# Buffers placed by the time they die, a shorter last routing and column-half sums in a kernel of pooled attention and soft mixture of experts

## The chip, the core and the metric

The kernel runs on one core of a Trainium2 chip. A core has a matrix engine (PE), a vector engine (DVE), an activation engine (ACT), a general engine (POOL), a queue that issues transfers (SP), and 16 DMA engines which all transfers share. The metric is the device time of one execution in microseconds; lower is better.

## What is computed

Everything is float32. Attention goes over 32 memory slots which are pooled from 576 tokens for each of 8 x 8 heads; its output is never formed for its own sake, but goes through a mixture of 8 experts with 4 slots each.

```python
a    = softmax(phi, axis=tokens)                # phi: 8 x 8 x 576 x 32
k_m  = einsum('bhsm,bhsd->bhmd', a, k)          # k, v: 8 x 8 x 576 x 64
v_m  = einsum('bhsm,bhsd->bhmd', a, v)
attn = softmax(q @ k_m.T / 8, axis=-1)
x    = (attn @ v_m) as 4608 tokens x 512
logits = x @ moe_phi                            # 4608 x 32
d    = softmax(logits, axis=tokens);  slot_input = d.T @ x      # 32 x 512
slot_out[e] = relu(slot_input[e] @ w1[e]) @ w2[e]               # 8 experts, 512 -> 1024 -> 512
out  = softmax(logits, axis=slots) @ slot_out   # 4608 x 512
```

The weights w1 and w2 are 32 MiB of the 66.65 MB that are read; the output is 9.44 MB.

## The kernel before

All work is added to a list (`add`, L45) with an engine, an estimated cost, the tiles that it reads and writes, and a priority. `Plan.order` (L77) plays the list through with these costs and writes out one order for each engine; nothing is reordered on the chip, so each engine and the SP queue work in that order.

**Attention.** The loop at L926 goes over four pairs of batches (`bp`). A pair loads phi, k, v and q, pools k and v (`pool_phi`, `pool_kv`), and for each of four head groups c does `scores` (L708, products at L716), `softmax` (L737, its result transposed at L777 into a tile of `aTs`) and `logits` (L780, product at L785), all summed into one PSUM bank `lp`. L955 transposes that bank into `L[bp]`.

**Routing.** `route` (L795) takes one pair's logits: a maximum over tokens (reduce L803, PE transpose L810, reduce L815, PE transpose L821), its subtraction (L829) and exp (L837) into `df`; the routing product L849 of `df` with the attention weights `ex` (a tile of `sexs`) and a column of ones; two copies of the result into `wt` on ACT (L861, L865); products L875 and L881 (the second gives the pair's sum of exponentials); a mask on DVE (L890) into `wtb`; and the product L909 with the pooled values `vm`. The pair's maximum goes to `MB` (L834), its sum to `SD` (L901), its slot sums to `SIU` (L922). After the last pair the four results are merged (L969 to L1000): scale by exp of the maximum's difference, add, divide, and write `SIM`, the input of the experts.

**Fills.** `fill` (L472) adds matmuls on ones whose result nobody reads. Twelve of them (L961, `NTAIL`) may go into gaps of PE once the third pair's maximum is there. On the profile they are L476.

**Experts.** `expert_in` (L1088, product L1097) runs w1 of eight experts, `hidden` the relu and a transpose into `hTb` (zeroed by POOL at L1050), `expert_out` (L1135, product L1148) w2. A weight tile is 1 MiB, two for each matrix. The products of `expert_out` accumulate in one PSUM bank over 512 columns; the last tile (`last`, L1139) comes in four quarter loads of 256 KB, and its two column halves go to spare parts of the banks. `slot_sums` (L1063) copies the accumulator to SBUF in column halves (L1070 on DVE, L1075 on ACT) and adds its four partition groups with a product (L1080); it runs once for all but the last tile and once for the last. Then `sr` is formed (L1266, L1271), and the output is products L1280 of the token softmaxes `cT` with `sr`, copies L1302, L1304, L1333, L1335 out of PSUM and transfers L1313 and L1343. `slots` (L1191) forms the token softmaxes, one pair after every second expert.

**Buffers.** Attention tiles live in one arena of 44,288 columns, stacked from the bottom in the order of the `stack` calls (L370 to L395). The 19 weight slots of 2048 columns (`ws`, L1025) lie over the same columns from 5376 up. A load into a slot waits for the last use of every attention tile under it, and for the planner a slot opens only when every tile of the pools under it has been handed out. Two more weight tiles use the area of q (`wqs`). SP issues the loads at L458.

Of the kernel before, what the change touches and what calls it, by code (L numbers as in the profile page):

```python
# [235 lines left out]
def act(n, psum=True):  # L236
    return (0.16 if psum else 0.19) + n / 1200.0
# [15 lines left out]
def kernel(  # L253
# [103 lines left out]
    def stack(shape, n, fifo=False):  # L357

        nonlocal top
        p = area(top, shape, n, (), fifo)  # L360

        p.aps.reverse()
        p.ranges.reverse()
        early.append(p)
        top += sum(c for _, c in p.ranges)
        return p


# [8 lines left out]
    dfs = stack([JN], 2)  # L377
    wts = stack([2, H * M + 1], 2)
# [17 lines left out]


# [10 lines left out]
    NTAIL = 12  # L408
# [31 lines left out]
    dmhs = sb("dmh", [NS, 1], 2)  # L440
    L = [keep(f"L{i}", [P, JN]) for i in range(NBP)]
# [353 lines left out]
    def route(bp, ex, vm):  # L795

        dm1, dmh, df = dm1s.tile(), dmhs.tile(), dfs.tile()
# [36 lines left out]
        add(ACT, act(32), lambda: nc.scalar.copy(MB.ap[:, bp, :], t1.ap[:, :NS]), r=[t1], w=[mbp])  # L834
# [4 lines left out]
        )  # L839
        wp = [b_m.tile(), b_m.tile()]  # L840
        wt, wtb = wts.tile(), wtbs.tile()
# [16 lines left out]
        add(PE, 1.3, f, r=[df, ex], w=wp, also=[wt])  # L858
# [7 lines left out]

        for g in range(2):
            add(ACT, act(HM) + act(1), lambda f=f, g=g: f(g), r=[wp[g]], w=[wt.part(g)])
        wtp = b_m.tile()

        def f():
            for g in range(2):
                for a in range(2):
                    x = NS * (2 * g + a)
                    nc.tensor.matmul(  # L875
                        wtp.ap[:, x: x + NS],
                        wt.ap[:, g, P * a: P * a + P],
                        rep[:, 0, :], start=True, stop=True,
                    )
            for g in range(2):  # L880
                nc.tensor.matmul(  # L881
                    wtp.ap[:, 4 * NS: 5 * NS],
                    wt.ap[:, g, HM: HM + 1].to_broadcast([P, P]), rep[:, 0, :],
                    start=(g == 0), stop=(g == 1),
                )

        add(PE, 1.3, f, r=[wt, rep_b], w=[wtp], also=[wtb])
        add(
# [10 lines left out]
        add(  # L899
            ACT, act(32),  # L900
            lambda: nc.scalar.copy(SD.ap[:, bp, :], wtp.ap[:, 4 * NS: 5 * NS]),  # L901
            r=[wtp], w=[SD.part(bp)],
        )
# [14 lines left out]
        if bp == NSEG - 1:  # L918
            return sip
# [6 lines left out]
    for bp in range(NBP):  # L926
# [22 lines left out]
        for c in range(C):  # L949
# [4 lines left out]
        add(  # L954
            DVE, dve(JN), lambda lp=lp, bp=bp: nc.vector.transpose(L[bp].ap, lp.ap[:, :JY]),  # L955
            r=[lp], w=[L[bp]],
        )
        plan.at(bp + (1.2 if bp < NBP - 1 else 1.0), 10)
        sip = route(bp, ex, vm)
    plan.at(20)  # L960
    fill(NTAIL, FILL + 1, [MB.part(NSEG - 2)])  # L961
# [3 lines left out]
    st = keep("st", [P, NS])  # L965
    nl = NSEG - 1

    def f():
        nc.vector.tensor_reduce(m4.ap, MB.ap.rearrange("p b n -> p n b"), axis=AX.X, op=ALU.max)  # L969
# [4 lines left out]
    add(DVE, 0.8, f, r=[MB], w=[m4, cf])  # L974
    add(ACT, act(NS * NSEG, False), lambda: nc.scalar.activation(cf.ap, cf.ap, AF.Exp), r=[cf], w=[cf])
# [9 lines left out]
    add(DVE, 2.6, f, r=[cf, SIU], w=[SIU, sip_c])  # L985

    def f():
        nc.vector.tensor_mul(sds.ap, SD.ap, cf.ap)
        nc.vector.tensor_reduce(st.ap, sds.ap.rearrange("p b n -> p n b"), axis=AX.X, op=ALU.add)
        nc.vector.tensor_scalar(st.ap, st.ap, EPS, None, op0=ALU.add)  # L990
        nc.vector.reciprocal(st.ap, st.ap)

    add(DVE, 1.2, f, r=[SD, cf], w=[sds, st])

    def f():
        bc = lambda x: x.unsqueeze(1).to_broadcast([P, DC, NS])
        last = sip.ap[:, :P].rearrange("p (c n) -> p c n", n=NS)
        nc.vector.tensor_mul(SIT.ap, last, bc(cf.ap[:, nl]))
        nc.vector.tensor_add(SIT.ap, SIT.ap, sip_c.ap)
        nc.vector.tensor_mul(  # L1000
            SIM.ap.rearrange("p c (e x) -> p c e x", e=E)[:, :, :, :SE],
            SIT.ap.rearrange("p c (e s) -> p c e s", e=E),
            bc(st.ap).rearrange("p c (e s) -> p c e s", e=E),
        )

    add(DVE, 0.8, f, r=[cf, st, sip, sip_c], w=[SIT, SIM])
# [14 lines left out]
    hTs, acs = over([8 * E * (NS + SE)], 1), over([DM], 2)  # L1021
# [28 lines left out]
    add(POOL, 2.0, lambda: nc.gpsimd.memset(hTb.ap, 0.0), r=[SIM], w=[hTb])  # L1050
# [8 lines left out]
    accs = [acs.tile().split(2) for _ in range(2)]  # L1059
# [3 lines left out]
    def slot_sums(x):  # L1063
        for d in range(2):
            cols = slice(d * HD, d * HD + HD)
            src = lambda d=d, cols=cols: pacc.ap[:, 0, cols] if x == 0 else pacc.ap[:, 1 - d, :HD]
            dst = lambda cols=cols: accs[x].ap[:, cols]
            if d == 0:
                add(
                    DVE, dve(HD), lambda src=src, dst=dst: nc.vector.tensor_copy(dst(), src()),  # L1070
                    r=[pacc.part(0) if x == 0 else pacc.part(1 - d)], w=[accs[x].part(d)],
                )
            else:
                add(
                    ACT, act(HD), lambda src=src, dst=dst: nc.scalar.copy(dst(), src()),  # L1075
                    r=[pacc.part(0) if x == 0 else pacc.part(1 - d)], w=[accs[x].part(d)],
                )
            add(
                PE, 0.5,
                lambda d=d, dst=dst: nc.tensor.matmul(  # L1080
                    so[d].ap, rep.rearrange("p a n -> p (a n)"), dst(),
                    start=(x == 0), stop=(x == 1),
                ),
                r=[accs[x].part(d), rep_b], w=[so[d]],
            )

# [48 lines left out]
    def expert_out(e):  # L1135
        w2v = w2[e].rearrange("(j p t) d -> p j (t d)", j=4, t=2)
        w2h = w2[e].rearrange("(j p t) d -> p j t d", j=4, t=2)
        for i in range(2):
# [18 lines left out]
            if not last:  # L1157
# [4 lines left out]
                add(  # L1162
                    PE, 0.9,
                    lambda mult=mult, i=i: mult(
                        pacc.ap[:, 0], 0, DM, e == 0 and i == 0, e == E - 1
                    ),
                    r=[hTb.part(e // EG), t], w=[pacc.part(0)],
                )
                if e == E - 1:
                    fill(2, FILL + 7, [t])  # L1170
# [8 lines left out]
            slot_sums(0)  # L1179
            for d in range(2):  # L1180
                add(
                    PE, 0.5, lambda d=d, mult=mult: mult(pacc.ap[:, 1 - d], d * HD, HD, True, True),
                    r=[hTb.part(e // EG), t.part(2 * d), t.part(2 * d + 1)], w=[pacc.part(1 - d)],
                )
# [105 lines left out]
    for d in range(2):  # L1290
        x = slice(d * HD, d * HD + HD)
        for i in range(G):
# [6 lines left out]
            def f(po=po, i=i, d=d):  # L1299
                dst = ot0.ap[:, i * DM + d * HD: i * DM + d * HD + HD]  # L1300
                if i % 2 == d:
# [5 lines left out]
                *((ACT, act(HD)) if i % 2 == d else (DVE, dve(HD))), f,  # L1307
# [72 lines left out]
```

## Time and profile before

| what | value |
|---|---|
| runs | 216.16, 216.18, 221.99 us |
| median | 216.18 us |
| profiled execution | 219.04 us |
| its span, first to last instruction | 217.2 us |
| mean granted PE clock | 0.918 |

Busy time over the span is 175.2 us for PE, 131.7 for DVE, 70.0 for ACT and 86.6 for POOL. The row DMA of the page gives the mean busy share of the 16 DMA engines in 40 slices of 5.43 us, in tenths; the rows after it are what they moved in GB/s, and the transfer queue's total.

```profile
DMA  6999999999999999999889979499999995059997
GB/s 214 386 392 391 380 393 375 390 381 392 385 388 389 385 408 347 393 391 388 322 293 414 367 269 400 118 410 345 409 404 410 408 407 195 5 199 416 414 413 295
q1 hardware_dynamic: 28960, 76.09, 92.8%
```

Attention's loads end near slice 20; weights fill the rest up to slice 33, and the output begins in slice 35. In the other views a row gives start and duration in us, engine, line, operation, output and input tiles, shape and count; a float32 matmul leaves two records. "idle before" names what ended the engine's wait. The rows of stretches give busy time of each engine, then granted PE clock, DMA share and GB/s.

### The profile page before, as it was taken

To read this page: it belongs to the slowest core of one execution; us is meant where nothing else is said; L and a number is where in the kernel's file an instruction comes from. 1 tells how busy PE (TensorE), PEld (TensorE's weight loads), DVE (VectorE), ACT (ScalarE), POOL (GpSimd) and SP (SyncE) were. 2 spreads that over 40 slices of the span, in tenths; PEclk is the share of its full clock that TensorE was granted. 3 is DMA by queue.
4 is the path that set the end of the run, shared out by engine and by line. 5 is a ranking of instruction groups with operands and counts; after the bars stand their busy time and mean duration, and the time that the engine had idled before them with its cause. 6 is when DMAs were issued, how large, how long until landed. Compare 5 with 4: busy or idle time off the path is not lost.

```text
span 217.2 us, 5728 instructions
## 1 busy us (share of the span) xinstructions
PE 175.2 (81%) x2462; PEld 108.8 (50%) x2462; DVE 131.7 (61%) x226; ACT 70.0 (32%) x186; POOL 86.6 (40%) x85
## 2 busy tenths in 40 slices
PE   8798977696598997969889799777999995899600
PEld 6576754465474574455565368543553331366200
DVE  6835047969539999967964995459300750189600
ACT  2042234443423726134742332020100321267500
POOL 6298009697952795399932484200000000000000
PEclk9999999859579999799997999996999999999955
DMA  6999999999999999999889979499999995059997
GB/s 214 386 392 391 380 393 375 390 381 392 385 388 389 385 408 347 393 391 388 322 293 414 367 269 400 118 410 345 409 404 410 408 407 195 5 199 416 414 413 295
DMA packets 28985, 76.45 MB, mean 352 GB/s; under 512 B 1824, under 2 KB 6944, under 8 KB 28960
## 3 DMA queue, kind: packets, MB, share of 16 engines
q1 hardware_dynamic: 28960, 76.09, 92.8%
q8 instruction: 19, 0.31, 0.6%
q14 instruction: 6, 0.05, 0.1%
HBM read 66.65 MB, written 9.44 MB: 350 GB/s over the span
## 4 chain that ended last, share of the span: by engine, by line
PE 40%; DMA 22%; DVE 13%; POOL 9%; issue 6%; ACT 3%; SPq 1%; DVEq 1%; POOLq 0%; ACTq 0%
DMA top<-in_q_dram 10%; DMA arena<-in_moe_w_dram 9%; PE kvbank L476 7%; PE bank L1097 6%; PE bank L785 5%; PE scbank L716 5%; PE kvbank L599 4%; PE bank L1280 3%; DMA out_dram<-arena 3%; DVE arena L700 3%; POOL arena L562 3%; POOL arena L774 3%; PE bank L849 2%; POOL arena L751 2%; DVE arena L511 2%
## 5 line engine op out<-in xcount | busy, mean ns | idle before, releaser
L549 POOL TENSOR_TENSOR arena<-arena 128x1152 f32<-128x1152 f32 x8 | 21.0, 2631 | 17.4 <-ACT arena L544 14.7
L476 PE MATMUL kvbank<-ones 128*128 128x256 f32 x96 | 26.2, 411 | 2.2 <-ACT arena L622 1.1
L700 DVE STREAM_TRANSPOSE arena<-top 128x1152 f32<-128x1152 f32 x16 | 21.7, 1358 | 7.0 <-DMA top<-in_q_dram 7.0
L716 PE MATMUL scbank<-arena 64*64 64x288 f32 x256 | 22.5, 447 | 3.0 <-DVE arena L730 2.5
L774 POOL TENSOR_TENSOR arena<-arena,ssm 128x576 f32<-128x576 f32 x16 | 18.4, 1158 | 15.6 <-DVE ssm L770 15.6
L562 POOL TENSOR_TENSOR arena<-arena 128x128 f32<-128x128 f32 (+2 forms) x32 | 23.4, 730 | 2.3 <-ACT arena L555 0.3
L599 PE MATMUL kvbank<-arena 64*32 64x128 f32 x1152 | 20.7, 278 | 4.3 <-ACT arena L555 2.7
L785 PE MATMUL bank<-arena 128*128 128x288 f32 x64 | 21.8, 475 | 2.0 <-DVE arena L777 2.0
L751 POOL TENSOR_TENSOR arena<-arena,smx 128x576 f32<-128x576 f32 x16 | 18.4, 1158 | 12.3 <-DVE smx L746 12.3
L476 PEld LDWEIGHTS kvbank<-ones 128*128 128x128 f32 x96 | 18.2, 202 | 7.7 <-issue 2.5
L599 PEld LDWEIGHTS kvbank<-arena 64*32 64x32 f32 x1152 | 16.5, 107 | 8.4 <-issue 3.8
L511 DVE TENSOR_REDUCE arena<-arena 128x128 f32<-128x1152 f32 x8 | 17.1, 2143 | 5.1 <-DMA arena<-in_phi_dram 5.1
L1148 PE MATMUL kvbank<-arena 128*32 128x512 f32 (+1 forms) x136 | 15.6, 573 | 3.8 <-DMA arena<-in_moe_w_dram 2.6
L730 DVE STREAM_TRANSPOSE arena<-scbank 128x576 f32<-128x576 f32 x16 | 12.2, 764 | 9.2 <-PE scbank L716 9.1
L785 PEld LDWEIGHTS bank<-arena 128*128 128x128 f32 x64 | 12.7, 215 | 7.5 <-DVE arena L777 3.0
L777 DVE STREAM_TRANSPOSE arena<-arena 128x576 f32<-128x576 f32 x16 | 12.2, 760 | 5.2 <-POOL arena L774 5.0
L1097 PE MATMUL bank<-arena,SIM 128*32 128x256 f32 x224 | 13.9, 409 | 1.7 <-DVE SIM L1000 1.7
L1280 PE MATMUL bank<-sr,cT 64*128 64x512 f32 (+1 forms) x78 | 14.6, 417 | 0.4 <-DVE sr L1271 0.2
L716 PEld LDWEIGHTS scbank<-arena 64*64 64x64 f32 x256 | 9.3, 139 | 11.1 <-DVE arena L730 4.1
L756 ACT ACTIVATE arena<-arena 128x576 f32<-128x576 f32 x16 | 11.0, 686 | 8.7 <-POOL arena L751 8.6
L1335 DVE COPY arena<-bank 128x512 f32<-128x512 f32 x17 | 11.5, 690 | 2.6 <-DMA out_dram<-arena 1.6
L1280 PEld LDWEIGHTS bank<-sr,cT 64*128 64x128 f32 x78 | 9.3, 184 | 5.7 <-DVE arena L1335 3.2
(111 smaller groups left out, 233.7 us busy)
## 6 DMA issues: line engine op xcount, KB each, us to landing
arena<-in_moe_w_dram SPq DMA_DIRECT2D x29, 1024.0 KB, 9.1
top<-in_q_dram SPq DMA_DIRECT2D x8, 1152.0 KB, 13.6
arena<-in_k_dram SPq DMA_DIRECT2D x8, 1152.0 KB, 10.7
arena<-in_v_dram SPq DMA_DIRECT2D x8, 1152.0 KB, 13.2
out_dram<-arena SPq DMA_DIRECT2D x11, 768.0 KB, 7.6
arena<-in_phi_dram SPq DMA_DIRECT2D x8, 576.0 KB, 8.2
top<-in_moe_w_dram SPq DMA_DIRECT2D x2, 1024.0 KB, 7.1
arena<-in_moe_w_dram SPq DMA_DIRECT2D x4, 256.0 KB, 15.4
```

Source lines behind the costliest of these rows:

```text
L476: lambda: nc.tensor.matmul(warm.ap, ones, ones.unsqueeze(1).to_broadcast([P, 2, P]), start=True, stop=True,),
L511: lambda: nc.vector.tensor_reduce(mx.ap, ph().rearrange("p c j m -> p c m j"), axis=AX.X, op=ALU.max),
L549: lambda: nc.gpsimd.tensor_tensor(ph(), ph(), mb.ap.unsqueeze(2).to_broadcast([P, C, J, M]), op=ALU.subtract),
L562: plus = lambda o, x, y: nc.gpsimd.tensor_tensor(o, x, y, op=ALU.add)
L599: nc.tensor.matmul(acc.ap[M * c: M * c + M, a, : 2 * D], ph()[h0: h0 + HALF, c, j, :], kv()[h0: h0 + HALF, :, c, j * D: j * D + D], start= ...
L700: nc.vector.transpose(qT.ap.rearrange("p (i u y) -> p u i y", i=2, y=Y), qt.ap[:, h * QT_SZ: h * QT_SZ + QT_SZ].rearrange("p (u i x) -> p ...
L716: nc.tensor.matmul(scb.ap[HALF * g: HALF * g + HALF, a, :JY], kb[g].ap[h0: h0 + HALF, i, c].rearrange("p r m -> p (r m)"), qT[g][c // 2].a ...
L751: lambda: nc.gpsimd.tensor_tensor(exv(), exv(), bc(mx), op=ALU.subtract),
L774: lambda: nc.gpsimd.tensor_tensor(exv(), exv(), bc(sm), op=ALU.mult),
L785: nc.tensor.matmul(lp.ap[:, :JY], vpb.ap[:, h, :], aT.ap[:, a * JY: (a + 1) * JY], start=(h == 0), stop=(h == H - 1),)
L1097: nc.tensor.matmul(hb.ap[NS * j: NS * j + NS, :256], SIM.ap[:, 2 * i + c, NS * e: NS * e + NS], wv[:, c, 256 * j: 256 * j + 256], start=(e ...
L1280: nc.tensor.matmul(po.ap[:, : x.stop - x.start], cT[bp].ap()[y: y + HALF, j // 2 * P: j // 2 * P + P], sr.ap[y: y + HALF, t, x], start=(t ...
```

## The change

There are three parts.

*Placement.* `stack` no longer gives addresses; `place` does, in a written order: at the bottom what the last merge and routing use, then upwards what dies earlier, kvs on top as before. The `dfs` and `wts` pools become one pool for each parity of the pair. `acs` shrinks to one tile; the number and addresses of the weight slots stay the same. The zeroing of `hTb`, whose columns now lie under routing tiles, moves from POOL to DVE, and is added behind SIM.

*The last pair's routing.* The first three pairs use the old steps under the name `weigh`. The last uses `weigh_last`: one maximum over all slots and tokens of a partition is read from the logits' PSUM bank, spread with a product and a minimum of the negated values, exp is taken straight out of PSUM with this as bias, and the result is transposed. The logits themselves are transposed into `L[3]` only after SIM. One of the two copies into `wt` goes to DVE, L881's product goes ahead of L875's, the merge of the first three pairs is formed while the last routing runs, and the division is folded into one factor. Twelve fills that followed the routing become three ahead of it, with seven single or double fills tied to its steps.

*Column halves.* Every w2 product is split into two halves of 256 columns, each with a bank of its own (`pacc.part(d)`), through all experts; `slot_sums` runs once. Two fills late in the experts go away. The token softmaxes come after experts 0 to 3 instead of 1, 3, 5 and 7, and two of the first output copies change engines.

```diff
+    def place(order):
+        nonlocal top
+        for p, i in order:
+            if p.aps[i] is None:
+                p.aps[i], p.ranges[i] = shaped(top, p.shape)
+                top += p.ranges[i][1]
...
-    dfs = stack([JN], 2)
-    wts = stack([2, H * M + 1], 2)
+    dfs = [stack([JN], 1) for _ in range(2)]
+    wts = [stack([2, H * M + 1], 1) for _ in range(2)]
...
+    place([
+        x for xs in (
+            every(MB), every(SD), every(cf), every(sds), every(SIU), every(sip_c), every(SIT),
+            every(wtbs), ((wts[1], 0),), ((dfs[1], 0),), every(vms), ((sexs, 1),), ((vpbs,
+            1),), every(aTs), every(dm1s), every(sexs), every(wts[0]), every(dfs[0]),
+            every(vpbs), ((kbs, 3),), ((kbs, 2),), every(kps), every(trees),
+            every(pmxs), every(pmbs), every(pess), every(mphi_b), every(vTs),
+            every(qTs), every(kbs), every(phis), every(kvs),
+        ) for x in xs
+    ])
...
-    NTAIL = 12
+    NTAIL = 3
...
+    def weigh_last(bp, lp):
+        dT, df = L[bp], dfs[bp % 2].tile()
+        def f():
+            nc.vector.tensor_reduce(dmx.ap[:, 0:1], lp.ap[:, :JY], axis=AX.X, op=ALU.max)
+            nc.vector.tensor_scalar(dmx.ap[:, 1:5], neg_b.ap, dmx.ap[:, 0:1], None, op0=ALU.mult)
+        add(DVE, dve(JN) + 0.15, f, r=[lp, neg_b], w=[dmx])
+        t0 = b_m.tile()
...
+            lambda: nc.tensor.matmul(
+                t0.ap[:, :C], rep.rearrange("p a n -> p (a n)"), dmx.ap[:, 1:5],
+                start=True, stop=True,
+            ),
...
+            lambda: nc.vector.tensor_reduce(dmx.ap[:, 5:6], t0.ap[:, :C], axis=AX.X, op=ALU.min),
...
+            lambda: nc.scalar.activation(dT.ap, lp.ap[:, :JY], AF.Exp, bias=dmx.ap[:, 5:6]),
...
+        add(DVE, dve(JN), lambda: nc.vector.transpose(df.ap, dT.ap), r=[dT], w=[df])
+        t1 = b_m.tile()
...
+        fill(1, FILL + 1, [lp])
+        fill(1, FILL + 2, [t0])
+        fill(2, FILL + 3, [t1])
...
+            if bp == NSEG - 1 and g == 1:
+                add(DVE, dve(HM) + dve(1), lambda g=g: f_dve(g), r=[wp[g]], w=[wt.part(g)])
...
+    def f():
+        nc.vector.tensor_mul(rst.ap[:, 0], wtp.ap[:, 4 * NS: 5 * NS], cf.ap[:, nl])
+        nc.vector.tensor_add(rst.ap[:, 0], rst.ap[:, 0], st.ap)
+        nc.vector.reciprocal(rst.ap[:, 0], rst.ap[:, 0])
+        nc.vector.tensor_mul(rst.ap[:, 1], rst.ap[:, 0], cf.ap[:, nl])
+        nc.vector.tensor_mul(sip_c.ap, sip_c.ap, bc(rst.ap[:, 0]))
...
+        nc.vector.tensor_mul(SIT.ap, part, bc(rst.ap[:, 1]))
+        nc.vector.tensor_add(
             SIM.ap.rearrange("p c (e x) -> p c e x", e=E)[:, :, :, :SE],
             SIT.ap.rearrange("p c (e s) -> p c e s", e=E),
...
+    keep_logits([SIM])
...
-    add(POOL, 2.0, lambda: nc.gpsimd.memset(hTb.ap, 0.0), r=[SIM], w=[hTb])
+    add(DVE, 2.4, lambda: nc.vector.memset(hTb.ap, 0.0), r=[SIM], w=[hTb])
...
-                add(
-                    PE, 0.9,
-                    lambda mult=mult, i=i: mult(
-                        pacc.ap[:, 0], 0, DM, e == 0 and i == 0, e == E - 1
-                    ),
-                    r=[hTb.part(e // EG), t], w=[pacc.part(0)],
-                )
-                if e == E - 1:
-                    fill(2, FILL + 7, [t])
+                for d in range(2):
+                    add(
+                        PE, 0.5,
+                        lambda d=d, mult=mult, i=i: mult(
+                            pacc.ap[:, d], d * HD, HD, e == 0 and i == 0, False
+                        ),
+                        r=[hTb.part(e // EG), t], w=[pacc.part(d)],
+                    )
...
-            slot_sums(0)
...
-        if e % 2 == 1:
-            slots(e // 2)
-    slot_sums(1)
+        if e < NBP:
+            slots(e)
+    slot_sums()
```

More of the change, by code (lines that the diff above doesn't have):

```diff
@@ L357, in stack @@
     def stack(shape, n, fifo=False):
-        nonlocal top
[L360 to L366, printed above, removed]
+        p = Slots([None] * n, [None] * n, (), fifo)
+        p.shape = shape
+        early.append(p)
+        return p
+    def place(order):
+        nonlocal top
+        for p, i in order:
+            if p.aps[i] is None:
+                p.aps[i], p.ranges[i] = shaped(top, p.shape)
+                top += p.ranges[i][1]
+        assert top <= ARENA and all(a is not None for p in early for a in p.aps)
     NSEG = NBP
@@ L395, with every @@
     kvs = stack([KV_SZ], 2, fifo=True)
+    def every(p):
+        p = p.pool if isinstance(p, Tile) else p
+        return [(p, i) for i in reversed(range(len(p.aps)))]
+    place([
[8 more added lines that the diff above has]
+    ])
     ident_b = keep("ident", [P, P])
@@ L833, in route @@
         )
-        add(ACT, act(32), lambda: nc.scalar.copy(MB.ap[:, bp, :], t1.ap[:, :NS]), r=[t1], w=[mbp])
+        add(
+            ACT, act(32),
+            lambda: nc.scalar.activation(MB.ap[:, bp, :], t1.ap[:, :NS], AF.Copy, scale=-1.0),
+            r=[t1], w=[mbp],
+        )
         add(
@@ L879, in f @@
                     )
[L880 to L884, printed above, removed]
-                )
         add(PE, 1.3, f, r=[wt, rep_b], w=[wtp], also=[wtb])
+        if bp == NSEG - 1:
+            fill(1, FILL + 5, [wtp])
         add(
@@ L898, in route @@
         )
-        add(
[L900 to L903, printed above, removed]
+        if bp < NSEG - 1:
+            add(
+                ACT, act(32),
+                lambda: nc.scalar.copy(SD.ap[:, bp, :], wtp.ap[:, 4 * NS: 5 * NS]),
+                r=[wtp], w=[SD.part(bp)],
+            )
         sip = b_m.tile()
@@ L1058, with slot_sums @@
     HD = DM // 2
-    accs = [acs.tile().split(2) for _ in range(2)]
+    accs = acs.tile().split(2)
     sr = keep("sr", [P, 2, DM], dtype=F32R, parts=2)
     so = [Tile(ap=scbank[:, d, :HD]) for d in range(2)]
-    def slot_sums(x):
+    def slot_sums():
         for d in range(2):
[L1065 to L1077, printed above, removed]
+            x = slice(d * HD, d * HD + HD)
+            add(
+                *((ACT, act(HD)) if d else (DVE, dve(HD))),
+                lambda d=d, x=x: (nc.scalar.copy if d else nc.vector.tensor_copy)(
+                    accs.ap[:, x], pacc.ap[:, d, :HD]
+                ),
+                r=[pacc.part(d)], w=[accs.part(d)],
+            )
             add(
                 PE, 0.5,
-                lambda d=d, dst=dst: nc.tensor.matmul(
-                    so[d].ap, rep.rearrange("p a n -> p (a n)"), dst(),
-                    start=(x == 0), stop=(x == 1),
+                lambda d=d, x=x: nc.tensor.matmul(
+                    so[d].ap, rep.rearrange("p a n -> p (a n)"), accs.ap[:, x],
+                    start=True, stop=True,
                 ),
-                r=[accs[x].part(d), rep_b], w=[so[d]],
+                r=[accs.part(d), rep_b], w=[so[d]],
             )
```

131 lines of the change are left out of this document (97 added, 34 removed).

## The prediction

> **What bounds the kernel now.** I read the DMA share over the span first, then busy time by stretch, the issues of the SP queue in order of time, and last the chain of waits in the two places where the transfers stop.
>
> ```profile
> 122.50:129.00 6.50, 5.02 (x67) 2.43 (x60) 6.33 (x13) 2.46 (x11) 4.43 (x5) 1.00 0.77 253
> 135.50:139.50 4.00, 4.00 (x18) 2.90 (x16) 1.76 (x3) 0.00 (x0) 0.00 (x0) 1.00 0.26 42
> 139.50:147.00 7.50, 4.08 (x58) 2.83 (x57) 4.15 (x11) 1.80 (x8) 2.02 (x1) 1.00 0.96 384
> 147.00:148.50 1.50, 0.36 (x4) 0.20 (x8) 1.40 (x6) 0.00 (x0) 0.00 (x0) 0.68 0.87 175
> 148.50:181.75 33.25, 31.52 (x392) 13.60 (x384) 12.61 (x33) 5.73 (x18) 0.00 (x0) 0.96 1.03 404
> 192.75:215.75 23.00, 11.66 (x60) 7.22 (x58) 10.99 (x17) 8.73 (x16) 0.00 (x0) 0.78 1.01 410
> ```
>
> The last three columns are granted clock, share of the 16 DMA engines, and GB/s. Transfers are the bound: they run at 404 to 410 GB/s through the weights and the output, so in this half of the span time is lost only where they stop. At 410 GB/s, from 111 us to 148.5 they lost 6.5 x (1 - 253/410) = 2.5, 4 x (1 - 42/410) = 3.6, 0.5 and 0.9: 7.5 us. Then the weights run from 148.5 to 181.75 without a stop, and the output fills 23 us from 192.75 on; between the two only stragglers move. A gain must shorten the holes before 148.5 or the hole before 192.75.
>
> **Placement of the buffers.** One 1 MiB weight tile (1.05 MB) takes 2.56 us at 410 GB/s. Of 32, 21 can be loaded before the experts run (19 arena slots, 2 in the q area); the other 11 need slots that expert matmuls give back. When is a slot free?
>
> ```profile
> 120.68 0.37 SPq L458 DMA_DIRECT2D arena<-in_moe_w_dram  x1
> 126.22 0.88 SPq L458 DMA_DIRECT2D arena<-in_moe_w_dram  x2
> 138.02 0.89 SPq L458 DMA_DIRECT2D arena<-in_moe_w_dram  x2
> 146.54 0.37 SPq L458 DMA_DIRECT2D arena<-in_moe_w_dram  x1
> 150.13 1.74 SPq L458 DMA_DIRECT2D arena<-in_moe_w_dram  x2
> ```
>
> Adding up the buffer sizes gives what lies under each 2048-wide slot. Before, slots come free in this order: last pair's c=1 scores, 1 slot; its c=3 scores, 2; pair 2's routing product, 1; last logits, 2 (aTs); last routing product, 1; wtbs read, 1; SIM, 1. The issues above show the first (120.68), second (126.22), fourth (138.02) and sixth (146.54) of these at their releases; 150.13 is the first slot given back by the experts. By the new addresses the same nine are: c=1 scores 2 (120.7), c=3 scores 3 (126.2), pair 2's wts read 2 (about 131.2), last logits 1, last routing product 1 (sexs[1]), and none waits for wtbs or SIM. Each comes ahead of the end of the queue before it. From 111 us, 13.8 tiles outstanding take 13.8 x 2.56 = 35.3, so traffic runs unbroken to about 146.4. Then all slots are full and DMA stands until the first expert tile is given back; placement alone gains no more than that.
>
> **The last pair's routing.**
>
> ```profile
> 134.23 0.78 DVE L777 STREAM_TRANSPOSE arena<-arena 128x576 f32<-128x576 f32 x1 [0.89 <-POOL arena L774]
> 135.34 0.78 DVE L777 STREAM_TRANSPOSE arena<-arena 128x576 f32<-128x576 f32 x1 [0.34 <-POOL arena L774]
> 133.19 2.86 PE L476 MATMUL kvbank<-ones 128*128 128x256 f32 x12
> 135.88 2.10 PE L785 MATMUL bank<-arena 128*128 128x288 f32 x8
> 138.02 0.48 DVE L955 STREAM_TRANSPOSE L<-bank 128x288 f32<-128x288 f32 x1 [1.90 <-PE bank L785]
> 139.28 0.27 PE bank L810
> 140.81 0.45 ACT L837 ACTIVATE arena<-arena 128x288 f32<-128x288 f32 x1
> 141.36 1.67 PE bank L849 x36
> 143.06 0.37 ACT L861 COPY arena<-bank 128x256 f32<-128x256 f32 x1 [1.06 <-PE bank L849]
> 143.51 1.06 PE bank L875 x8
> 144.57 0.46 PE bank L881 x4
> 145.05 0.70 DVE arena L890
> 145.80 0.67 PE L909 MATMUL bank<-arena 128*64 128x128 f32 x8 [0.78 <-DVE arena L890]
> 146.94 0.35 DVE st L991
> 147.79 0.30 DVE SIM L1000
> 148.00 0.45 DVE L1198 TENSOR_REDUCE cmx<-L 128x9 f32<-128x288 f32 x1
> ```
>
> From the last logits (137.98) to SIM (148.09) is 10.1 us. Four parts:
> - Fills, 12 to 3: six of the old twelve (12 records from 133.19, two to a fill) held c=2's logits to 135.88 though their input was there at 135.01. The first three go into earlier gaps, so none is left here: logits of c=2 run at 135.05 and of c=3, half of 2.10 each, from 136.15 to 137.4, 0.6 earlier. Without that cover the clock may fall; see the rivals.
> - Logits end to routing product: 3.38 us before (transpose, reduce, transpose, reduce, transpose, subtract, exp). After: a reduce of 288 (0.45, from L1198), the 4-wide scaling (unseen; 0.1 to 0.48, taken 0.15 as so narrow), a small matmul (0.27), a reduce of 4 (0 to that 0.45; 0.2), exp out of PSUM (0.45, ends 0.3 to 0.6), transpose (0.48), and hand-overs of 0.03 to 0.05, 0.25 in all: 2.25. Fills sit in that line on PE; 0.15 for one that overruns (0 to 0.5). 2.4 in all, ends 2.0 to 3.0: 1.0 gained.
> - Routing product 139.8 to 141.5; copies on ACT and DVE side by side, 0.37 and a one-column copy, but DVE may still be in the merge sums formed ahead: 0.75 (before 0.45); L881 and L875 1.52, to 143.8; L890 to 144.55. The ahead-of-time products of SIU sit under those matmuls on DVE; without that cover they cost 1.2.
> - Merge: before, 2.35 from L890's end to SIM. After: five DVE steps (three of 32 columns at an estimated 0.18, under the 0.30 of 128; the 0.35 reciprocal; one of 128), 1.3 with hand-overs, under which L909's 0.67 hides, then two at 0.3: 1.9. SIM at 146.45: 1.65 earlier, ends 0.4 to 2.4.
>
> The memset of hTb goes from POOL, where it lay beside the routing, to DVE behind SIM: 3.1 us at the 0.78 per 576 columns above, and the kept transpose 0.48. PE needs hTb only after 8 expert tiles of about 1 us, so both are hidden; if not, they delay the first token softmaxes, which have 30 us.
>
> **From SIM to the end of the weights.**
>
> ```profile
> 113.41:116.82 3.41, 3.31 (x10) 2.31 (x10) 2.11 (x4) 1.00 (x6) 1.16 (x1) 0.50 1.02 407
> 144.13:147.54 3.41, 1.55 (x16) 1.20 (x15) 2.10 (x7) 0.18 (x1) 0.00 (x0) 1.00 0.97 381
> 147.54:150.95 3.41, 2.81 (x28) 1.38 (x32) 3.09 (x9) 0.44 (x1) 0.00 (x0) 0.50 1.00 327
> 150.95:154.36 3.41, 3.41 (x68) 1.88 (x64) 3.12 (x8) 0.44 (x1) 0.00 (x0) 1.00 1.03 406
> ```
>
> The expert matmuls start at half clock (0.50), so the first slot comes back 2.0 us after SIM (150.13). The spread fills fill the stretch of 1.55 us busy; at full clock 16 records take 16 x 3.41/68 = 0.8, with drain 1.1. First slot at 147.55, traffic again 1.5 later as after the issue at 138.02: 149.05. Eleven tiles, less a trailing 0.15 MB, at 404 GB/s take 28.2: bulk done 177.2 against 181.75, 4.6 earlier. (The holes say the same: 7.5 less 2.6 is 4.9.)
>
> By the Trainium skill (TensorE: Matmul & The Clock Gate, Part 1) the gate watches a free-running window of about 3.4 us; the two cold stretches here are each 3.41 long and lie ten such lengths apart, so the trace agrees. The same page ("Why this matters for your kernels") lets idle gaps under about 3 us pass; the trace does not bear that out, as 1.55 us of work in 3.41 was enough to fall cold. By the page the gap the removed fills leave is free and 208.6 stands; by the trace it may cost the 1.2 of the first rival.
>
> **Column halves.**
>
> ```profile
> arena<-in_moe_w_dram SPq DMA_DIRECT2D x1, 256.0 KB, 10.7
> 174.52 2.32 SPq L458 DMA_DIRECT2D arena<-in_moe_w_dram  x1
> 185.13 0.38 ACT arena L1075
> 187.25 0.57 PE kvbank L1148 x8
> 189.01 0.61 PE scbank L1080 x2
> 190.51 0.44 DVE sr L1271
> 191.90 1.34 SPq L1313 DMA_DIRECT2D out_dram<-arena  x3
> ```
>
> The last quarter is issued at 174.52 and lands at 185.2; its matmul ran at 187.25 since fills, a first pair of sums and copies out of the shared bank stood ahead of it. First output issue: 191.90, 6.7 after landing. After: last half product 0.6, ACT copy 0.38, slot sum 0.61, sr copy 0.38, subtract 0.44, hand-overs 0.25, then 0.91 to the issue as from 190.99 now: 3.6, with 0.1 for ACT's column-0 copies. 3.0 gained, ends 2.2 to 3.4. Twice as many half-width products per tile (2 x 0.57, taken as 1.2) fit in 2.56 us. Token softmaxes at experts 0 to 3 move within the same cover.
>
> **Sum.** 4.6 + 3.0 = 7.6 off the profiled execution's 219.04 (span 217.2 and 1.84 around it). It lies 2.86 above the median of the runs; I take the same 7.6 from the median: 216.18 - 7.6 = 208.6. With the ends above (SIM 0.8 earlier or 1.2 later than taken, tail 0.4 and 0.8) its own range is 207.4 to 210.6.
>
> **Rivals.** *The clock falls elsewhere.* With three fills PE idles from 133.2, where the six began, to 135.05; and late in the experts it has only 1.2 us of work per 2.56.
>
> ```profile
> 110.00:113.41 3.41, 2.43 (x31) 2.06 (x22) 2.09 (x6) 0.92 (x5) 0.60 (x1) 1.00 0.93 350
> 113.51 2.29 PE L785 MATMUL bank<-arena 128*128 128x288 f32 x4 [0.28 <-DVE arena L777]
> ```
>
> For: 2.43 busy of 3.41 was followed by a cold window, and logits took 2.29 there instead of 1.05. Against: dense products filled windows as thin in the experts and stayed at 1.00. Price: 2.29 less 1.05, so 1.2, at the logits (209.8), or in the tail about 1.5 for half-clock half product, sum and first output (210.1); both 211.3. *Placement frees nothing early* (the planner keeps the old issue order): the holes shrink only by what the routing gains, 1.5, and 4.5 remain: 211.7. For it: issue order is the planner's; against: it issued each freed slot at once before. *Slower: the SP queue blocks.* Issues are in order; if a load over sexs[1] stands ahead, those behind it wait for the last routing product (141.5) and start at 143. With k tiles held, the last 11 start at 143 + 2.56k, against 153.55 now; less the tail's 3.0, it costs from k = 6 on, over 2% from k = 7, and all nine give 225.7. Against: every issue above followed its release.
>
> **Chances.** Forecast 0.60, clock 0.22 (210.0), no early frees 0.08 (211.7), blocked queue 0.05 (over 220), and 0.05 for all gains at their upper ends (under 206.4). Range 206.4 to 211.9: it drops the blocked queue, the upper ends and part of the third. 2% of 216.18 is 4.3, about what a measurement of this kernel tells from no change: faster means under 211.86. That takes forecast, clock, upper ends less a little, 0.86; same 0.09; slower 0.05.
>
> **What would show it.** Loads at 120.7 (2), 126 (3), 131 (2); no DMA hole from 111 to 146, then one of about 2.6 us; the routing product near 139.8, SIM near 146.5; granted clock 1.00 at the first expert product; first slot back 1.1 us after SIM; first output 3.6 us after the last quarter lands. It is wrong if the hole at 146 is over 4 us, if 0.50 shows around 134 to 141 or in the tail, or if the output starts over 4.5 us after landing.

## The result and the profile after

| kernel | runs | median, us | ratio to before (95%) |
|---|---|---|---|
| before, same chip | 4 | 216.51 | 1 |
| changed | 4 (211.16 to 212.26) | 212.06 | 0.9754 (0.9719 to 0.979) |

The change is faster, by 2.5%: 5.3 us of the 216.18 that the prediction started from, with ends of 4.5 and 6.1. It had forecast 7.6. The ratios here and below are recorded for the fast executions and are not the quotients of the medians beside them (here 212.06/216.51 = 0.979). The profiled execution took 211.16 us, its span 209.4, the mean granted clock was 0.946.

First, on the page of the changed kernel, the rows of the 40 slices (5.24 us each now) for granted clock and GB/s.

```profile
PEclk9999999969979999999996999999999999969965
GB/s 206 369 391 391 380 390 380 390 382 386 389 380 393 385 395 408 378 389 392 407 311 408 415 394 394 407 410 250 308 408 412 405 410 286 3 270 414 414 413 295
```

Before, slices 23, 24 and 26 (counted from 1) fell to 367, 269 and 118 of some 400; now the traffic holds from slice 22 through 27, and one hole is left in slices 28 and 29. The hole ahead of the output (slice 35, with 3 GB/s) has not gone, and PEclk stands at 6 in slice 36, where the output starts. The issues of the SP queue in order of time say when the slots came free:

```profile
119.16 0.88 SPq L484 DMA_DIRECT2D arena<-in_moe_w_dram  x2
124.72 1.39 SPq L484 DMA_DIRECT2D arena<-in_moe_w_dram  x3
129.54 0.37 SPq L484 DMA_DIRECT2D arena<-in_moe_w_dram  x1
130.08 0.37 SPq L484 DMA_DIRECT2D arena<-in_moe_w_dram  x1
135.94 0.37 SPq L484 DMA_DIRECT2D arena<-in_moe_w_dram  x1
140.59 0.37 SPq L484 DMA_DIRECT2D arena<-in_moe_w_dram  x1
146.19 3.27 SPq L484 DMA_DIRECT2D arena<-in_moe_w_dram  x3
```

Two, three, two, one and one: the nine slots of the prediction in its order, and then the first slot that the experts give back. Rows of the stretch where the slots run out (the last three columns are clock, DMA share and GB/s):

```profile
144.00:145.00 1.00, 0.66 (x4) 0.26 (x2) 0.93 (x6) 0.00 (x0) 0.00 (x0) 1.00 0.78 311
145.00:146.00 1.00, 0.94 (x20) 0.60 (x24) 0.56 (x3) 0.00 (x0) 0.00 (x0) 1.00 0.24 74
146.00:147.00 1.00, 1.00 (x24) 0.60 (x20) 1.00 (x1) 0.00 (x0) 0.00 (x0) 1.00 0.18 74
147.00:148.00 1.00, 1.00 (x24) 0.63 (x20) 1.00 (x2) 0.00 (x0) 0.00 (x0) 1.00 0.90 102
148.00:149.00 1.00, 1.00 (x28) 0.57 (x23) 0.93 (x3) 0.29 (x1) 0.00 (x0) 1.00 0.92 356
```

At 410 GB/s these five lose 0.24 + 0.82 + 0.82 + 0.75 + 0.13 = 2.8 us, where 2.6 was forecast. From the chain of waits, the last pair's routing (last logits, routing product, SIM):

```profile
133.57 2.36 PE bank L811 x8
138.88 1.60 PE bank L939 x36
144.71 0.30 DVE SIM L1123
```

From the logits' end at 135.93 to SIM at 145.01 it takes 9.08 us, 10.11 before. And the chain from the last tile to the output:

```profile
178.14 0.44 DVE arena L1192
178.62 0.78 PE kvbank L1266 x8
179.40 0.64 PE scbank L1199 x2
180.07 0.38 ACT sr L1382
180.49 0.71 PE scbank L1199 x2
181.23 0.44 DVE sr L1387
181.69 0.38 ACT sr L1382
182.09 0.44 DVE sr L1387
```
```profile
183.48 2.10 SPq L1429 DMA_DIRECT2D out_dram<-arena  x3
```

The last quarter was issued at 167.92 and took 10.8 us to land; the product at 178.62 starts within 0.1 us of that, and is counted as the landing. The first output left at 183.48, 4.86 later. Forecast were 3.6. The two halves do not run side by side: the second sum (180.49) stands behind the first half's copy (180.07), and its copy (181.69) behind the first half's subtraction.

Cut into pieces, the two profiled executions (219.04 and 211.16 us, 7.9 apart) differ so:

| piece | before | after | saved | forecast |
|---|---|---|---|---|
| start to last logits' end | 137.98 | 135.93 | 2.05 | 0.6 |
| logits' end to SIM | 10.11 | 9.08 | 1.03 | 1.05 |
| SIM to first slot's issue | 2.04 | 1.18 | 0.86 | 0.9 |
| first slot's issue to last quarter landed | 35.07 | 32.43 | 2.64 | 2.05 (the 4.6 less the three above) |
| landed to first output issue | 6.70 | 4.86 | 1.84 | 3.0 |
| first output issue to end | 25.34 | 25.87 | -0.53 | 0 |

The sum of the forecast holds between these two executions (7.6 against 7.9), but its pieces at both ends don't, and the medians differ by less. The experiments follow these three questions.

### The profile page after: what moved, and what is told of

It reads as the page before. It is cut to its first block, busy times and chain, and to the rows that moved or that the text cites. A ratio compares the mean times of both kernels' runs of the same rounds, so it can differ in the third digit from the quotient of the medians.

```text
span 209.4 us, 5942 instructions
## 1 busy us (share of the span) xinstructions
PE 171.1 (82%) x2571; PEld 109.9 (52%) x2571; DVE 133.6 (64%) x232; ACT 69.6 (33%) x183; POOL 84.4 (40%) x84
## 4 chain that ended last, share of the span: by engine, by line
PE 38%; DMA 22%; DVE 15%; POOL 10%; issue 5%; ACT 2%; SPq 2%; DVEq 1%; POOLq 0%; ACTq 0%
DMA top<-in_q_dram 10%; DMA arena<-in_moe_w_dram 9%; PE kvbank L502 5%; PE bank L811 5%; PE scbank L742 5%; PE bank L1215 5%; PE bank L1396 4%; PE kvbank L625 4%; POOL arena L800 3%; DVE arena L726 3%; DMA out_dram<-arena 3%; POOL arena L588 3%; PE bank L939 2%; POOL arena L777 2%; POOL arena L575 2%
## 5 line engine op out<-in xcount | busy, mean ns | idle before, releaser
L502 PE MATMUL kvbank<-ones 128*128 128x256 f32 x88 | 25.7, 427 | 2.2 <-ACT arena L648 1.1
L742 PE MATMUL scbank<-arena 64*64 64x288 f32 x256 | 21.7, 433 | 3.0 <-DVE arena L756 2.5
L502 PEld LDWEIGHTS kvbank<-ones 128*128 128x128 f32 x88 | 17.1, 209 | 7.0 <-issue 2.1
L811 PEld LDWEIGHTS bank<-arena 128*128 128x128 f32 x64 | 11.9, 205 | 10.3 <-DVE arena L803 6.1
L1266 PE MATMUL kvbank<-arena 128*32 128x256 f32 x256 | 16.1, 382 | 1.1 <-DMA arena<-in_moe_w_dram 0.6
L1396 PE MATMUL bank<-sr,cT 64*128 64x512 f32 (+1 forms) x78 | 15.6, 459 | 0.3 <-DVE sr L1387 0.2
L742 PEld LDWEIGHTS scbank<-arena 64*64 64x64 f32 x256 | 9.1, 137 | 10.8 <-DVE arena L756 4.5
L1396 PEld LDWEIGHTS bank<-sr,cT 64*128 64x128 f32 x78 | 10.6, 209 | 5.2 <-DVE arena L1451 3.4
L1215 PE MATMUL bank<-arena,SIM 128*32 128x256 f32 x224 | 12.5, 380 | 0.4 <-DVE SIM L1123 0.4
```

The costliest lines, as they stand in the source:

```text
L502: lambda: nc.tensor.matmul(warm.ap, ones, ones.unsqueeze(1).to_broadcast([P, 2, P]), start=True, stop=True,),
L742: nc.tensor.matmul(scb.ap[HALF * g: HALF * g + HALF, a, :JY], kb[g].ap[h0: h0 + HALF, i, c].rearrange("p r m -> p (r m)"), qT[g][c // 2].a ...
L811: nc.tensor.matmul(lp.ap[:, :JY], vpb.ap[:, h, :], aT.ap[:, a * JY: (a + 1) * JY], start=(h == 0), stop=(h == H - 1),)
L1215: nc.tensor.matmul(hb.ap[NS * j: NS * j + NS, :256], SIM.ap[:, 2 * i + c, NS * e: NS * e + NS], wv[:, c, 256 * j: 256 * j + 256], start=(e ...
L1396: nc.tensor.matmul(po.ap[:, : x.stop - x.start], cT[bp].ap()[y: y + HALF, j // 2 * P: j // 2 * P + P], sr.ap[y: y + HALF, t, x], start=(t ...
```

## The experiments

**What the parts are worth, and what the kernel before does when it runs again.** `again` is the kernel before, unchanged. `place` has the placement alone, `route` the last pair's routing with merge and fills, `halves` the column halves with the token softmaxes and output copies; hTb is zeroed by POOL in all of them.

The core of `place`, which has the whole order of the change's diff:

```diff
-    dfs = stack([JN], 2)
+    dfs = [stack([JN], 1) for _ in range(2)]
...
+    place([
```

Of `route`:

```diff
-    NTAIL = 12
+    NTAIL = 3
...
+    def weigh_last(bp, lp):
```

Of `halves`:

```diff
-    accs = [acs.tile().split(2) for _ in range(2)]
+    accs = acs.tile().split(2)
...
-        if e % 2 == 1:
-            slots(e // 2)
+        if e < NBP:
+            slots(e)
```

> The kernel before, unchanged. My theory: the profiled execution of before (219.04) was 2.9 above its median because of where its half-clock stretches of the matrix engine fell (41.9 to 48.7, 55.6 to 62.1, 86.5 to 89.7, 113.4 to 116.8, 147.5 to 151.0), so another profile of it lies near 216.5 with other or fewer such stretches before 110 us, and its last logits end 1 to 2 us earlier than 137.98. Rival: the 2.9 is the same in every profile (a cost of profiling), then the profile is again near 219 with the logits' end near 138.0.

> Only the placement of the buffers (with the two pools by parity); routing, fills, column halves as before. My theory: transfers run without a hole from 111 us until all 21 slots are full, near 146 to 147, then stand until the experts give a slot back at half clock; worth about 2.0 us, because the slots and not the placement limit it. Rival 1 (parts add up, placement carries most): 4 us or more. Rival 2 (the transfers were hidden anyway): under 0.5 us.

> Only the last pair's routing, the merge ahead and the fills; old placement, old expert sums. My theory: SIM comes about 1.6 us sooner after the last logits' input and the first slot back about 1.1 instead of 2.0 us after SIM, but slots under wtbs, sexs and SIM still open late, so 1.5 us of it reaches the end. Rival (the routing is hidden behind weight transfers in the old placement): under 0.5 us. Rival (all of it reaches the end): 2.6 us.

> Only the expert part: column halves, one slot sum, token softmaxes earlier, output copies on other engines. My theory from the profile of the changed kernel: first output issue 4.9 instead of 6.7 us after the last quarter lands, given back in part where the matrix engine falls to half clock at the start of the output: 1.2 to 1.8 us. Rival (the prediction's 3.0 stands): 3.0 us. Together, if the three parts add up to less than the whole change's 5.3, placement and routing need each other.

| kernel | median, us (runs) | ratio (95%) |
|---|---|---|
| again | 219.14 (12: 216.34 to 220.8) | 1.0013 (0.9962 to 1.0064) |
| place | 216.84 (12) | 0.9947 (0.9907 to 0.9987) |
| route | 218.26 (12) | 1.0024 (0.9985 to 1.0063) |
| halves | 216.0 (6) | 0.9895 (0.984 to 0.9951) |

Eight of these twelve runs of the kernel before lie between 216.3 and 219.5 us, the other four from 220.1 to 220.8. In the profile of `again` (216.72 us, span 214.9) the c=1 scores give their slot back at 119.69, where the profile before had 120.68, and the issues and the chain from there to SIM are alike:

```profile
119.69 0.37 SPq L458 DMA_DIRECT2D arena<-in_moe_w_dram  x1
```

From that issue to the last logits' end it is 17.30 us in both. So the 1.5 us by which the changed kernel reaches this point earlier (119.16) are not the change's: nothing ahead of it was made shorter, and the kernel before gets 1.0 of them by itself. The point goes with the half-clock windows ahead of it. In `after_pool` below, which is the change but for one memset, these begin at 43.7, 54.0, 84.7 and 112.0 us, in `again` at 43.6, 53.9, 84.6 and 111.9, and the slot comes back at 119.68 in the one and at 119.69 in the other. Behind it the changed kernel takes 16.77, 0.53 less: that is what the removed fills gave (0.6 forecast).

`place` and `route` were expected to save 2.0 and 1.5 us. They save 0.5% (1.1 us) and nothing that can be told from zero. Their traces show a reason. First `place`, on POOL and DVE, then `route`:

```profile
144.55 2.02 POOL L1069 MEMSET arena<- 128x2304 f32 x1 [11.34 <-PE bank L928]
...
144.68 1.92 DVE L1009 TENSOR_SCALAR st<-st 128x32 f32<-128x32 f32 x1
```
```profile
137.58 2.02 POOL L1155 MEMSET arena<- 128x2304 f32 x1 [2.17 <-PE bank L792]
...
138.05 1.57 DVE L860 TENSOR_SCALAR dmx<-neg,dmx 128x4 f32<-128x4 f32 x1
```

The same two steps where no memset runs, in `place_dve` below and in the changed kernel:

```profile
145.53 0.18 DVE L1009 TENSOR_SCALAR st<-st 128x32 f32<-128x32 f32 x1
```
```profile
136.44 0.23 DVE L879 TENSOR_SCALAR dmx<-neg,dmx 128x4 f32<-128x4 f32 x1
```

A tensor-scalar that takes 0.18 us over 32 columns lasts 1.92, and one that takes 0.23 over 4 columns lasts 1.57. Both end within 0.03 us of POOL's memset (146.57 and 139.60). The zeroing of hTb held the vector engine on the path to SIM. In `place` logits' end to SIM takes 11.88 us, 1.77 more than before, and the hold is 1.74 of it. In `route` it is 11.94, 2.86 more than in the change: 1.34 by the hold, and PE, idle behind it from 137.94 to 139.68, then ran four fills and the routing product at half clock. From the chain of `route`:

```profile
140.94 2.00 PE kvbank L483 x4
142.94 2.00 PE bank L920 x36
```

In the changed kernel these take 1.06 and 1.60, so another 1.34 went there. The fills that were to hold the clock stood on the path themselves, and were slow. That the clock fell because PE stood idle behind the hold is an inference; `route_dve` below fits it.

**The memset.** `place_dve` and `route_dve` are the same two with the zeroing moved behind SIM on DVE, as in the change; `after_pool` is the change with it back on POOL; `after_again` is the change once more.

```diff
-    add(POOL, 2.0, lambda: nc.gpsimd.memset(hTb.ap, 0.0), r=[SIM], w=[hTb])
+    add(DVE, 2.4, lambda: nc.vector.memset(hTb.ap, 0.0), r=[SIM], w=[hTb])
```

> Placement and the zeroing of hTb moved to DVE behind SIM; nothing else. In the run of the placement alone the zeroing on POOL (144.55 to 146.57) held a DVE tensor_scalar of 32 columns from 144.68 to 146.60, so SIM came 1.7 us late. My theory: that wait goes, every expert step moves up 1.7, and since all slots were full long before, it reaches the end: 1.7 better than placement alone, 2.8 us better than before. Rival (transfers bound it anyway): no better than placement alone, 1.1 us.

> Routing, merge ahead and fills with the zeroing of hTb on DVE; old placement, old expert sums. In the run of the routing alone the zeroing on POOL (137.58 to 139.60) held the 4-wide scaling from 138.05 to 139.62 instead of 0.24. My theory: SIM comes 1.3 to 1.7 sooner than there; at most 1.5 better than before, as late slots still bound it. Rival (transfers bound all of it): equal to before within 0.4 us.

> The change, unchanged, beside the same runs of before. Theory: the measured ratio 0.9754 holds within its interval; the parts with the zeroing on DVE (2.8 and 1.5) and the halves (2.3) add to 6.6 at most, so about 5 to 6.5 us. The profile again shows a dry stretch of DMA near 145 to 148 and a first output issue 4.5 to 5 us after the last quarter lands; cold stretches lie elsewhere.

> The change with the zeroing of hTb left on POOL. Theory (POOL's memset holds only DVE operations of the kind of tensor_scalar and SBUF copies): here it runs once the last routing product with vm has been read, beside tensor_tensor and reduce steps, so SIM is not later: within 0.4 us of the change. Rival (POOL's memset slows every DVE operation, or the zeroing comes late for the experts): 1.0 us or more slower than the change.

| kernel | median, us (runs) | ratio (95%) |
|---|---|---|
| place_dve | 215.44 (6) | 0.989 (0.9844 to 0.9935) |
| route_dve | 215.14 (6) | 0.9898 (0.9863 to 0.9933) |
| after_again | 211.31 (5) | 0.9723 (0.9685 to 0.9762) |
| after_pool | 212.35 (6) | 0.977 (0.9728 to 0.9812) |

Routing with the memset moved is 1.0% faster than the kernel before (2.2 us, where at most 1.5 was expected), and its interval lies clear of `route`'s. In its trace logits' end to SIM takes 9.04 us, 2.9 less than in `route`, and PE stays at full clock: the hold and the slow stretch behind it are both gone, which is more than the 1.3 to 1.7 that was expected.

For the placement the intervals overlap (0.5% against 1.1%). Logits' end to SIM is 1.74 shorter in `place_dve` than in `place`, but the two profiled executions took the same time (215.06 and 215.10). `place_dve` was 0.9 later at the c=1 scores, and 0.8 went again behind SIM, where its half-clock window lasts 5.6 us into the experts, against 3.8. So of the 2.8 us that were expected against the kernel before, 2.4 are measured.

`halves` gives 1.05% (2.3 us, by its interval 1.1 to 3.5), which holds both the 1.2 to 1.8 that was expected and the rival's 3.0. With the memset moved, a part is worth about 1%: placement 1.1, routing 1.0, halves 1.05, together 3.2, and the whole 2.5 to 2.8. In the whole change the memset matters less, as its place falls elsewhere:

```profile
144.69 2.02 POOL L1174 MEMSET arena<- 128x2304 f32 x1 [10.36 <-PE bank L1014]
144.70 0.28 DVE L1115 TENSOR_TENSOR arena<-arena,rst 128x128 f32<-128x128 f32 x1
```

In `after_pool` it runs beside the last three tensor-tensor steps of the merge, the first of which is shown with its 0.28 us, and from the logits to SIM it is 9.08 us as in the change. Its interval overlaps that of `after_again`: there the move of the memset can't be told from nothing. The medians differ by 1.0, the size that the rival named, but of the 1.15 us between the two profiled executions 1.0 lies ahead of 119.7 us, before the memset. `after_again` confirms the change: 2.8%, or 6.0 us, where 5 to 6.5 were expected.

**The tail and the hole that is left.** Four kernels take the changed one further. `slot20` makes room for a twentieth weight slot (`sr` goes to where q was), so that a load need not wait for the first expert tile. `so` gives the second column half's slot sum a PSUM tile of its own. `tailfill` is `so` with fills in the gaps of the last sums, to hold the clock. `best` has all three.

```diff
-    ARENA = 44288
+    ARENA = 45312
...
-    so = [Tile(ap=scbank[:, d, :HD]) for d in range(2)]
+    so = [Tile(ap=scbank[:, 0, :HD]), b_l.tile()]
...
+            tail_fill(1, FILL + 8, [pacc.part(d)])
+            tail_fill(1, FILL + 9, [so[d]])
```

> The change with a twentieth weight slot: the arena grows by 1024 columns, and sr, which is needed only at the end, moves into the area that q has left. My theory: the dry stretch of about 2.6 us after all slots are full (near 145 to 148) is there because no slot is free; one more tile of 2.56 us fills it, so the end comes 2.0 to 2.6 us sooner than the change: a ratio of 0.960 to 0.963 to the kernel before. Rival (the end hangs on SIM alone, the eleven tiles behind it being bound by how fast slots come back): no gain, 0.972.

> The change with the slot sums of the two column halves in two PSUM banks that are different tiles instead of halves of one. My theory: the second sum waited for the copy of the first (0.55 us) and the subtraction of the first for the second sum, since both lie in one tile; apart, the first output issue comes 0.6 to 0.8 us sooner after the last quarter's landing (4.9 to about 4.2). Rival (the waits were for data): no change in that stretch.

> The run before this one with four single fills on a spare bank, tied to the column halves' products and sums. My theory: the output products start at full clock and the first 2 us of output run at full rate, 0.6 us in those executions in which they otherwise start at half clock. Rival (fills delay the sums by as much as the clock gives): no gain or a loss up to 0.5 us.

> The three edits together on the change: twentieth slot, two tiles for the sums, tail fills. If they work at different places they add: 3 to 4 us faster than the change, a ratio of 0.953 to 0.959 to the kernel before. Rival (the output's bandwidth or the weights bind in their place): under 2 us faster than the change.

| kernel | median, us (6 runs each) | ratio (95%) |
|---|---|---|
| slot20 | 210.68 | 0.9742 (0.9692 to 0.9792) |
| so | 211.0 | 0.9749 (0.9715 to 0.9783) |
| tailfill | 210.62 | 0.9744 (0.971 to 0.9778) |
| best | 209.81 (208.77 to 210.28) | 0.9693 (0.9654 to 0.9733) |

These ratios can be held against the change's only by their intervals, and these overlap for all four. Each step alone is therefore not shown by the times; the traces must say what it did.

In `so` the second half's sum no longer waits for the first half's copy. From its timeline:

```profile
179.74 0.70 PE L1199 MATMUL scbank<-arena,rep 128*128 128x256 f32 x2
...
180.29 0.70 PE L1199 MATMUL bank<-arena,rep 128*128 128x256 f32 x2
180.48 0.37 ACT L1382 CAST sr<-scbank 128x256 fp32r<-128x256 f32 x1 [0.24 <-PE scbank L1199]
...
182.93 0.37 SPq L1429 DMA_DIRECT2D out_dram<-arena  x1
```

The first output leaves 3.84 us after the last half product starts (179.09), against 4.86 in the change, so one tile shared by two halves cost 1.0 of the 1.3 that the tail missed. Expected were 0.6 to 0.8. What `so` does not recover is at the output's start. Three rows of the same stretch, of the change, `so` and `tailfill`:

```profile
184.00:187.00 3.00, 3.00 (x15) 2.24 (x11) 2.06 (x3) 1.55 (x3) 0.00 (x0) 0.56 0.73 272
```
```profile
184.00:187.00 3.00, 2.73 (x17) 1.20 (x16) 2.56 (x5) 2.34 (x5) 0.00 (x0) 1.00 0.73 272
```
```profile
184.00:187.00 3.00, 2.86 (x19) 1.33 (x17) 2.57 (x5) 2.29 (x5) 0.00 (x0) 1.00 1.03 397
```

The change moves 272 GB/s there at half clock, and `so` moves the same 272 at full clock, so the clock is not what holds the output back. What differs is the second output issue. In `again`, the change, `so` and `tailfill`, in this order:

```profile
190.05 0.38 SPq L1313 DMA_DIRECT2D out_dram<-arena  x1
```
```profile
183.94 1.16 SPq L1429 DMA_DIRECT2D out_dram<-arena  x1
```
```profile
183.40 1.52 SPq L1429 DMA_DIRECT2D out_dram<-arena  x1
```
```profile
183.49 0.38 SPq L1443 DMA_DIRECT2D out_dram<-arena  x1
```

All fourteen profiles divide by it. Where it takes 0.38 us (`again`, the kernel before, `place`, `place_dve`, `route`, `route_dve`, `tailfill`, `best`), the time from the first output issue to the end is 25.3 to 25.4 us. Where it takes 0.97 to 1.52 (`halves`, the change, `after_again`, `after_pool`, `slot20`, `so`), that time is 25.7 to 26.3, and only the change is at half clock there. So the loss comes with the column-half part, in which two output copies change engines; why the issue lasts longer is not shown, and putting those copies back was not tried. The tail fills shorten it again (25.4 in `tailfill`, after 26.3 in `so`), though not through the clock that they were meant for. They give some of it back in the sums (4.4 us from the last half product to the output, after 3.84), and the times of the two can't be told apart.

`slot20` was expected to gain the whole hole, 2.0 to 2.6 us. The hole is gone (348 to 422 GB/s in each us from 144 to 149), yet the first output leaves 37.06 us after SIM where the change takes 38.47 and `after_again` 37.95: 0.9 to 1.4 gained. Its stretch from the first expert product to the last half, and the end of its chain:

```profile
146.25:178.10 31.85, 31.75 (x528) 18.06 (x528) 15.19 (x37) 5.58 (x18) 0.00 (x0) 1.00 0.95 366
```
```profile
172.71 5.36 PE kvbank L1269 x96
178.10 0.43 DVE arena L1195
178.58 0.64 PE kvbank L1269 x8
```

PE is busy for 31.75 of 31.85 us, at full clock. The weights no longer set the end of the experts; the products do, and they can't start before SIM. From SIM's end to the end of the long row of products it takes 31.84 us (146.23 to 178.07), in the change 33.11 (145.01 to 178.12): 1.3 us, and there is nothing more to be had from earlier transfers. Some of the gain was lost again ahead of SIM in this execution, where the routing product of pair 2 fell into a window at half clock; `slot20` first, then `best`:

```profile
125.25 2.81 PE L939 MATMUL bank<-arena 64*32 64x288 f32 x36
```
```profile
125.01 1.67 PE L939 MATMUL bank<-arena 64*32 64x288 f32 x36
```

The chain of `slot20` also shows a second wait of the kind that `so` removes. The last quarter was issued at 166.22 and landed 10.9 us later, at 177.1, but the second half's product starts at 178.58, when the first half's copy out of the same tile (178.10, 0.43) is done. That costs 0.5 us; a tile for each half was not tried.

`best` is faster than the kernel before by 2.7 to 3.5%. Its slowest run (210.28) lies under the fastest of the changed kernel's nine (210.31), and its median 1.5 to 2.25 under theirs, though those nine were taken at other times. Expected were 3 to 4, and the rival's bound was under 2. Of what is missing, `slot20`'s part went to PE, and in the profiled execution another 1.2 to the clock: a half-clock window from 135.0 to 138.4 lies on the last logits, which take 2.96 us where the change has 2.36, and their end to SIM takes 9.67 where it has 9.08.

```profile
133.41 2.96 PE bank L811 x8
```

## Why the prediction was right in its range and 2 us out in its time

**Placement: right.** The nine slots came free in the predicted order and number, each 0.9 to 1.7 us ahead of the predicted times; the early part of this execution was 1.5 ahead by itself. Traffic ran unbroken from 111 to 144, and the hole behind it lost 2.8 us for 2.6. No load stood in front of an earlier one: the rivals of the blocked queue and of the planner's old order fall.

**The last routing: right in size, in part by luck, and one step priced at nothing that isn't.** Fills gave 0.53 for 0.6, logits' end to SIM 1.03 for 1.05, and the first slot came back 1.18 us after SIM for 1.1, at full clock. Inside the 1.03, though, two errors met. Logits' end to routing product took 2.95 where 2.4 was forecast: four fills held PE to 138.88, when the transposed input had been ready at 138.37. From the routing product to SIM it took 6.13 where the forecast had 6.65. The memset's move to DVE was costed as hidden, and the text asked only what it costs where it goes. What it saves where it leaves was left out: 1.7 us for placement alone, 1.3 and as much again in the clock for routing alone. This didn't hurt the forecast for the whole, where memset and tensor-scalar don't meet.

**Column halves: the right direction, mis-sized at 3.0.** The term measured 1.84. The list of steps (half product, copy, sum, copy, subtract) was taken for the second half alone, as if the first had left the way. On the chip both halves lie in one PSUM tile, so the first half's copy and subtraction stand inside the second half's chain. With a second tile the stretch is 3.84, near the 3.6 of the text. The prediction's own mark, "over 4.5 us after landing", was met by 4.86, and so was that of half clock in the tail (183.2 to 186.6).

**The clock rival: it fell in the tail and at the logits, but only the logits show a price.** It named half clock in the tail, with half product, sum and first output, for 1.5. In the changed kernel's profile only the output's start fell there, and the 0.5 that the output lost is lost at full clock too, as the second output issue shows; the prediction put the output's stretch at no change. At the logits it named 1.2. That window did not come in this execution, but it came in `best`, behind a window with 1.61 us of work in 3.40 (131.6 to 135.0), and cost 0.60 and 0.59, and the one before pair 2's routing product in `slot20` (1.1 us) is of its kind.

**The step that failed the time: the 7.6 taken from the median.** The prediction saw that its profile lay 2.86 above the median and took the profile's saving from the median all the same. The profile of `again`, 2.3 us shorter, shows what was in that surplus: 1.0 lies ahead of 119.7 us, and 1.2 between the first slot that the experts give back and the last quarter's landing (33.84 us, 35.07 before). The experts' start at half clock, in contrast, is no accident of one execution: `again`, `halves`, `place` and `place_dve` have it too, and get the first slot back 2.0 to 2.1 us after SIM, where every run with the new routing has 1.2.

Against `again` the pieces of the table come to 1.06, 1.03, 0.85, 1.41, 1.76 and -0.53, together 5.6 us, and the many runs show 2.5 to 2.8% of 216.18, or 5.3 to 6.0. By that measure the weights' stretch was put 0.6 too high (2.05), the tail 1.2 (3.0) and the output 0.5 (nothing). The agreement of 7.6 with 7.9 in the table is luck: the early part (1.5) and the weights (0.6) gave 2.1 that were not forecast, the tail and the output 1.7 less than forecast. The 1.5 is no work of the change; the tail's part belongs to it, and the output took as long (26.0) in the second run of the change and in `slot20`. By the ratio, 216.18 x 0.9754 = 210.9, the time lies within the range of 206.4 to 211.9; the median of 212.06 lies 0.2 above its end.

What stays open: how much of the difference between the sum of the parts, 3.2%, and the whole, 2.5 to 2.8%, is real. The intervals of the parts allow that there is none.

## What to carry to other kernels

Price a change against several executions of the kernel before, or cut the profile at a point ahead of the first changed instruction and count only what lies behind it: here 1.5 of 7.9 us lay ahead of it. Before a loss is put down to the clock, look for an execution with the same loss at full clock; `so` was one. Where a result is split so that its halves can overlap, look at whether both halves share one tile in every buffer on the way; one that is shared puts them in a row again. When a bound is loosened (here the transfers, by a slot more), work out at once how long the next one is busy in the same stretch: 31.75 of 31.85 us leaves nothing.

## What the runs showed of the hardware that was not expected

A memset on POOL held a tensor-scalar on DVE until it had ended: 1.92 us in place of 0.18, and 1.57 in place of 0.23. A tensor-tensor step beside such a memset took 0.28 us, as without one (0.29 in the change). The Trainium skill (GPSIMD Engine Reference, Specifications) says that POOL and DVE share their way into SBUF and contend where DVE runs in its fast two-port mode or with two inputs from SBUF. The traces agree that there is contention, but here the step with two SBUF inputs (144.70) was not slowed, and the other one lasted to the memset's end. Whether the tensor-scalar ran in that two-port mode, no run here shows.

Eight of twelve runs of unchanged code, the kernel before, spread from 216.3 to 219.5 us, and the same instructions fall into half-clock windows in one execution and not in the next: pair 2's routing product took 2.81 us in `slot20` and 1.67 in `best`.
